# Sorting the second batch's k and v in natural layout, with crossbar transposes in place of TensorE's

**Chip, cores, metric.** One core of one Trainium2 chip. The metric is the device time of one execution in microseconds (us), median of the fast runs (a run over 1.5% above the fastest of its kernel counts as slow), and only fast runs are compared. The span in a profile is some 2 us shorter than the time.

## The reference

Four batches of eight heads: a Sinkhorn-normalised 8 x 8 matrix per head mixes the eight blocks of k and of v, then softmax attention runs inside each block of 96 rows; the result goes through a feed-forward network (FFN).

```python
# q, k, v: (4, 8, 768, 64); sort_net: (4, 8, 8, 8)
P = sinkhorn(sort_net)                                   # five rounds
k_sorted = einsum('bhij,bhjcd->bhicd', P, k_blocks)      # v the same
attn = softmax(q_blocks @ k_sorted^T / 8)                # within a block of 96
x = (attn @ v_sorted) -> (3072, 512)
out = relu(x @ w_in)**2 @ w_out                          # 512 -> 2048 -> 512
```

## The kernel before

The FFN runs in eight tiles of 384 tokens, two to a batch of heads. The attention of a batch runs, in four pairs of heads, between the FFN matmuls of the batch before. A planner on the host (`Plan`) lays all instructions in order of a time model; the order on TensorE (PE), VectorE (DVE), ScalarE (ACT) and the DMA issuer SP is fixed by it. The loads are issued by GpSimd (POOL); there the framework chooses the order, and an instruction waits only for what it needs, not for the plan's time.

Two forms of attention exist. Batches 1 and 2 (`u.b` 0 and 1) sort with full matrices on TensorE and transpose q and sorted v there, and x too, except for the first three of batch 2's four x. Batches 3 and 4 sort k and v in natural layout with 32 x 32 tiles of TensorE, send v through DRAM for its re-tiling, and transpose k, q and x by crossbar DMA:

```python
def load(b, t, h0, n, p=slice(0, 128)):          # GpSimd DMA, casts to bf16
    ...                                          # natural rows for b > 1 and k, v
    dma(..., readers[b - 2] + [x_done[b - 1, x, 0] for x in range(HP)] if b > 1 else [])
    # the second list is seen by the planner alone; the chip waits for the buffer only

def s_nat(b, g, t, due):                         # sort two head pairs in tiles   (L632)
    ...
    wr = plan.add("SP", 0.33, write, evs + [loaded(b)])   # v to DRAM             (L656)
    there = plan.add("WAY", 2.0, ...)
    rd = plan.add("SP", 0.33, read, [there] + oldw)       # and back, re-tiled    (L662)

def s_turn(b, hp):
    sp = plan.add("SP", 1.25, k_turn, [op, loaded(b)] + oldx)   # crossbar        (L683)
    k_op = plan.add("WAY", 1.6, ...)
    qp = plan.add("DVE", 0.5, q_pair, ...)                # qi: ring of two       (L695)
    sp = plan.add("SP", 1.25, q_turn, [qp, loaded(b)] + oldq)   # crossbar        (L706)

def s_xt(u, due=0, eng=AD):
    if u.b > 1 or u.b == 1 and u.hp < HP - 1:             # crossbar              (L764)
        ...
    # else: four or eight transposes on TensorE and a copy    (L779)
```

The softmax here doesn't subtract the row's maximum and nothing guards it: scores larger than these inputs give would overflow.

## Time and profile before

| | before |
|---|---|
| time, us | 226.5 (226.37 to 226.66) |
| span of the profile, us | 224.3 |
| TensorE busy | 216.6 us, 97% |
| granted TensorE clock | full throughout |
| last load of batch 3 / of batch 4 landed | 63.0 / 87.7 us |
| start of the third FFN tile (first of the second batch) | 82.7 us |

"Landed" means that the transfer's completion was signalled.

### The profile page before, as it was taken

Reading aid. Unit: us, or ns where it says so; the run is one execution under the profiler, and the core shown is the slowest. Engines: PE = TensorE matmul, PEld = TensorE weight load, DVE = VectorE, ACT = ScalarE, POOL = GpSimd, SP = SyncE. Lnnn points to the kernel's source line nnn. Section 1 sums busy time; section 2 is a strip of 40 time slices with the busy share of each in tenths; the row PEclk is TensorE's granted clock in tenths of the full one; section 3 lists DMA queues with packets and bytes.
Section 4 is the critical chain, followed back from the end, with each engine's and each line's share of the span. In section 5 each row is a group of like instructions: output and inputs, shape, how many; then the busy total and the mean of one; then the engine's idle time right before and its main releaser. Section 6 shows DMA issues by size and latency. Waiting matters only on the chain.

```text
span 224.3 us, 5245 instructions
## 1 busy us (share of the span) xinstructions
PE 216.6 (97%) x2130; PEld 122.9 (55%) x2145; DVE 105.7 (47%) x297; ACT 122.1 (54%) x253; POOL 26.4 (12%) x46
## 2 busy tenths in 40 slices
PE   7898999999999999999999999999999999999994
PEld 2476665556665645545665455445665465446553
DVE  6777777317666416640666127523664045005400
ACT  4665776228885328734775248535774177137521
POOL 7962332200004200000000000000000000000000
PEclk9999999999999999999999999999999999999999
DMA  5999999999953996499941320899522410110012
GB/s 66 201 202 208 207 206 205 203 227 245 210 65 27 191 239 145 115 216 201 220 38 35 85 94 0 164 225 254 110 37 43 122 47 1 50 57 37 0 50 94
DMA packets 42744, 28.83 MB, mean 129 GB/s; under 512 B 22752, under 2 KB 38368, under 8 KB 42720
## 3 DMA queue, kind: packets, MB, share of 16 engines
q0 software_dynamic: 13888, 13.63, 37.1%
q1 hardware_dynamic: 28832, 14.86, 29.7%
q8 instruction: 17, 0.28, 0.5%
q14 instruction: 7, 0.06, 0.1%
HBM read 28.89 MB, written 7.91 MB: 164 GB/s over the span
## 4 chain that ended last, share of the span: by engine, by line
PE 92%; DMA 2%; DVE 2%; ACT 1%; issue 1%; ACTq 0%; POOLq 0%
PE hp L810 37%; PE op L838 35%; PE p L550 4%; PE p L731 3%; DMA qb<-in_q_dram 2%; PE p L510 2%; PE qtp L461 2%; PE vbp L598 2%; PE op L872 2%; PE p L350 1%; PE p L632 1%; PE xtp L779 1%; PE tp L510 1%; DVE ao L742 1%; ACT h L818 0%
## 5 line engine op out<-in xcount | busy, mean ns | idle before, releaser
L810 PE MATMUL hp<-xT,w_in_bf 128*128 128x384 bf16 x512 | 91.0, 326 | 0.0
L838 PE MATMUL op<-w_out_bf,h 128*128 128x512 bf16 x353 | 82.6, 379 | 0.8
L818 ACT ACTIVATE h<-hp 128x384 bf16<-128x384 f32 x128 | 62.0, 495 | 23.5 <-PE hp L810 20.0
L821 DVE TENSOR_TENSOR h<-h 128x384 bf16<-128x384 bf16 x128 | 44.5, 355 | 56.3 <-ACT h L818 55.5
L810 PEld LDWEIGHTS <-w_in_bf 128*128 128x128 bf16 x512 | 47.0, 98 | 30.0 <-issue 0.7
L838 PEld LDWEIGHTS <-h 128*128 128x128 bf16 x368 | 34.7, 98 | 39.4 <-issue 0.7
L192 ACT COPY ob<-op 128x512 f32<-128x512 f32 (+1 forms) x25 | 14.2, 569 | 56.0 <-PE op L838 50.6
L742 DVE TENSOR_TENSOR ao<-p,rec 96x512 bf16<-96x512 f32 x32 | 22.0, 687 | 1.4 <-DVE rec L741 0.3
L582 ACT ACTIVATE et<-p 96x384 bf16<-96x384 f32 x48 | 19.4, 491 | 2.4 <-PE p L550 2.4
L741 DVE RECIPROCAL rec<-p 96x8 f32<-96x8 f32 x32 | 6.4, 199 | 13.6 <-PE p L731 13.3
L731 PEld LDWEIGHTS <-et 96*128 96x128 bf16 x256 | 10.6, 97 | 2.9
L261 POOL DMA_DIRECT2D qb<-in_q_dram x8 | 6.0, 754 | 32.5 <-PE qtp L461 24.4
L350 PE MATMUL p<-ones 128*128 128x512 bf16 (+1 forms) x36 | 8.8, 360 | 1.1 <-DVE ones L213 1.1
L194 DVE COPY vs<-vbp 96x512 bf16<-96x512 bf16 (+1 forms) x12 | 6.1, 508 | 7.1 <-PE vbp L598 6.9
L573 ACT ACTIVATE et<-p 96x768 bf16<-96x768 f32 x8 | 6.3, 802 | 2.1 <-PE p L550 2.0
L261 POOL DMA_DIRECT2D kb<-in_k_dram x10 | 6.6, 659 | 6.6 <-DMA w_in_bf<-in_moe_w_in_dram 2.2
L261 POOL DMA_DIRECT2D vb<-in_v_dram x10 | 6.6, 660 | 6.4 <-DMA w_in_bf<-in_moe_w_in_dram 3.6
L192 ACT CAST ksT<-p 128x768 bf16<-128x768 f32 (+1 forms) x7 | 4.6, 662 | 3.3 <-PE p L510 3.3
L550 PEld LDWEIGHTS <-kx 64*128 64x128 bf16 x128 | 4.6, 155 | 2.8 <-issue 2.8
L731 PE MATMUL p<-vs,et 96*128 96x65 bf16 x128 | 6.0, 193 | 0.0
L461 PE MATMUL qtp<-ident,qb 64*64 64x64 bf16 (+1 forms) x144 | 4.7, 204 | 1.3 <-DMA qb<-in_q_dram 1.3
L461 PEld LDWEIGHTS <-qb 64*64 64x64 bf16 (+1 forms) x144 | 3.5, 109 | 4.5 <-DMA qb<-in_q_dram 2.3
(78 smaller groups left out, 129.3 us busy)
## 6 DMA issues: line engine op xcount, KB each, us to landing
out_dram<-ob SPq DMA_DIRECT2D x23, 256.0 KB, 2.8
qb<-in_q_dram POOLq DMA_DIRECT2D x8, 384.0 KB, 15.7
vb<-in_v_dram POOLq DMA_DIRECT2D x6, 384.0 KB, 17.1
kb<-in_k_dram POOLq DMA_DIRECT2D x6, 384.0 KB, 17.1
w_in_bf<-in_moe_w_in_dram POOLq DMA_DIRECT2D x4, 512.0 KB, 12.5
w_out_bf<-in_moe_w_out_dram POOLq DMA_DIRECT2D x4, 512.0 KB, 18.0
v_way<-vn SPq DMA_DIRECT2D x4, 396.0 KB, 4.1
vblk<-v_way SPq DMA_DIRECT2D x4, 396.0 KB, 3.9
```

Source lines behind the costliest of these rows:

```text
L192: nc.scalar.copy(out=out, in_=in_)
L261: nc.gpsimd.dma_start(out=dst, in_=src)
L350: nc.tensor.matmul(out=out, lhsT=ones, rhs=rhs, start=True, stop=True)
L461: nc.tensor.transpose(out=t["p"][64 * h:64 * (h + 1), a, :], in_=qb[p0:p1, 2 * hp + h, D * a:D * (a + 1)], identity=ident[p0:p1, p0:p1])
L550: nc.tensor.matmul(out=scp[:, h, BLK * n:BLK * (n + 1)], lhsT=(u.ksT[64 * h:64 * (h + 1), hf, BLK * n:BLK * n + 128] if u.b < 2 else kx_r[ ...
L582: nc.scalar.activation(out=et[:, h, 0:HS].rearrange("p (n c a) -> p n c a", c=C0, a=NA), in_=st["p"][0:96, h, 0:HS].rearrange("p (n a c) - ...
L731: nc.tensor.matmul(out=oup[:, h, 66 * n:66 * n + D + 1], lhsT=et_r[u.et[hf]][:, h, BLK * n:BLK * n + 128], rhs=(u.vs[:, NQ * hf + n, h, 0: ...
L742: nc.vector.tensor_tensor(out=u.ao[:, n0:n0 + NQ, :, :].rearrange("p n e d -> p e n d"), in0=ov[:, :, :, 0:D], in1=rec[:, :, :, None].to_b ...
L810: nc.tensor.matmul(out=t["hp", nt][:, 0:HS], lhsT=w_in_bf[:, kc, 128 * nt:128 * (nt + 1)], rhs=xT[:, kc, t0:t0 + HS], start=(kc == 0), sto ...
L818: nc.scalar.activation(out=t["h1", nt], in_=t["hp", nt][:, 0:HS], func=AF.Relu)
L821: nc.vector.tensor_tensor(out=t["h2"][:, nt, :], in0=t["h1", nt], in1=t["h1", nt], op=ALU.mult)
L838: nc.tensor.matmul(out=t["op", mt], lhsT=t["h2"][:, nt, 128 * mt:128 * (mt + 1)], rhs=w_out_bf[:, nt, :], start=(nt == 0), stop=(nt == NT ...
```

## The change

Batch 2 joins the form of batches 3 and 4. The intent is to take its transposes and full sorts off TensorE, which bounds the kernel. The core of the diff:

```diff
-            if b > 1 and t:
+            if b > 0 and t:                 # natural rows for batch 2's k and v too
...
-            for t in (2, 1, 0):
+            for t in (1, 2, 0):
                 load(1, t, HP * g, HP)
...
-        if u.b > 1 or u.b == 1 and u.hp < HP - 1:
+        if u.b > 0:                         # every x of batch 2 by crossbar
...
-                if b == 1:
-                    build_w(H * b + 2 * hp, 2, pt, kops[b - 1, hp])
...
-    lay(1, (0, 1), n_up, 2 * n_up)
-    lay_late(2, 2 * n_up)
-    lay_late(3, 4 * n_up)
+    todo.append((8, len(todo), build_wt, 0))
+    lay_late(1, (n_up - 5, n_up + 1), n_up + 6, 5)
+    for b in (2, 3):
+        c0 = 2 * (b - 1) * n_up
+        todo.append((c0, len(todo), lambda due, b=b: load_late(b), 0))
+        lay_late(b, (c0 + 9, c0 + 18), c0 + 25, 6)
```

The rest is `u.b < 2` becoming `u.b < 1` in scores and attention, and a ring of four k buffers for three.

More of the change, by code (lines that the diff above doesn't have):

```diff
@@ L177 @@
     rqT, rao, rks, ret = Ring(6), Ring(3), Ring(3), Ring(4)
-    rkx, rkn, rqi = Ring(3), Ring(3), Ring(2)
+    rkx, rkn, rqi = Ring(3), Ring(4), Ring(2)
     AD = ("ACT", "DVE")
@@ L235 @@
     v_way = nc.dram_tensor("v_way", (B, 2, NA, 128, HP * 66), BF16, kind="Internal").ap()
-    kn_r = [const.tile([128, NA, 2, D], BF16, name=f"kn{n}") for n in range(3)]
+    kn_r = [const.tile([128, NA, 2, D], BF16, name=f"kn{n}") for n in range(4)]
     qi_r = [const.tile([128, NA, 2, D], BF16, name=f"qi{n}") for n in range(2)]
@@ L252 @@
     xT = const.tile([128, KC, n_tok], BF16)
-    w_all = const.tile([128, NH // 2, NB, C0], BF16)
+    w_all = const.tile([128, H, NB, C0], BF16)
     w_t = const.tile([128, NH // 4, 4, NB], BF16)
@@ L436, in __init__ @@
             self.b, self.hp, self.halves = b, hp, halves
-            if b > 1:
+            if b > 0:
                 self.i0, self.ni, self.full = 0, NB, True
@@ L544, in mm @@
                 qT = tiles["qT", u.b, u.hp]
-                if u.b < 2:
+                if u.b < 1:
                     qT = qT.rearrange("p a x -> p (a x)").rearrange("p (i q) -> p i q", q=BLK)
@@ L552, in mm @@
                             lhsT=(u.ksT[64 * h:64 * (h + 1), hf, BLK * n:BLK * n + 128]
-                                  if u.b < 2 else
+                                  if u.b < 1 else
                                   kx_r[u.kx][64 * h:64 * (h + 1), NQ * hf + n::NB]),
-                            rhs=(qT[64 * h:64 * (h + 1), NQ * hf + n, :] if u.b < 2 else
+                            rhs=(qT[64 * h:64 * (h + 1), NQ * hf + n, :] if u.b < 1 else
                                  qT[64 * h:64 * (h + 1), :, C0 * (NQ * hf + n):
@@ L561, in s_sc @@
             u.et[hf], olde = ret.take()
-            pe = plan.add("PE", 0.17 if u.b < 2 else 0.26, mm, [u.k_op, u.q_op] + old, due,
+            pe = plan.add("PE", 0.17 if u.b < 1 else 0.26, mm, [u.k_op, u.q_op] + old, due,
                           mode="row")
@@ L565, in s_sc @@
             rqT.use(qTs[u.b, u.hp], pe)
-            if u.b < 2:
+            if u.b < 1:
                 rks.use(u.n, pe)
@@ L716, in s_av @@
         nao, olda = rao.take()
-        if u.b > 1:
+        if u.b > 0:
             w, u.vs_op = v_blk[u.b, u.hp // 2]
@@ L733, in mm @@
                             lhsT=et_r[u.et[hf]][:, h, BLK * n:BLK * n + 128],
-                            rhs=(u.vs[:, NQ * hf + n, h, 0:D + 1] if u.b < 2 else
+                            rhs=(u.vs[:, NQ * hf + n, h, 0:D + 1] if u.b < 1 else
                                  vb_r[w][:, NQ * hf + n, 2 * (u.hp % 2) + h, 0:D + 1]),
@@ L753, in s_av @@
             ret.use(u.et[hf], pe)
-            if u.b < 2:
+            if u.b < 1:
                 rks.use(u.n, pe)
@@ L761, in s_xt @@
     def s_xt(u, due=0, eng=AD):
-        if u.b > 1 or u.b == 1 and u.hp < HP - 1:
+        if u.b > 0:
             def turn(e):
@@ L956, in lay, with lay_late @@
                 todo.append((c + step * f, len(todo), s, b))
-    def lay_late(b, c0):
-        todo.append((c0, len(todo), lambda due: load_late(b), 0))
-        if b == 2:
-            todo.append((c0, len(todo), build_wt, 0))
+    def lay_late(b, nat, c1, step):
         for g in range(2):
             for t in (1, 2):
-                todo.append((c0 + 9 + 9 * g, len(todo),
-                             lambda due, g=g, t=t: s_nat(b, g, t, due), b))
+                todo.append((nat[g], len(todo), lambda due, g=g, t=t: s_nat(b, g, t, due), b))
         for hp in range(HP):
@@ L973, in scores @@
                 s_sc(u, due)
-            c = c0 + 25 + 6 * hp
+            c = c1 + step * hp
             todo.append((c, len(todo), scores, b))
```

## The prediction

> **What bounds the kernel now.** I read the page's busy shares first, then the chain of waits.
>
> ```profile
> PE 216.6 (97%) x2130; PEld 122.9 (55%) x2145; DVE 105.7 (47%) x297; ACT 122.1 (54%) x253; POOL 26.4 (12%) x46
> PE 92%; DMA 2%; DVE 2%; ACT 1%; issue 1%; ACTq 0%; POOLq 0%
> ```
>
> TensorE is busy 97% of 224.3 us and carries 92% of the chain that ends last. VectorE and ScalarE stand near half. So a microsecond taken off TensorE's in-order stream is a microsecond off the time, and each new wait in that stream is paid in full. What the change removes are pieces of that stream. The chain in order of time (start, us, what) gives one head pair of the second batch, then its last output transpose and two pieces that the third batch has instead:
>
> ```profile
> 62.52 0.46 PE qtp L461 x12
> 62.98 0.34 PE p L510 x12
> 64.07 0.46 PE p L510 x12
> 65.28 0.28 PE p L550 x8
> 65.58 0.35 PE p L550 x8
> 66.69 0.45 PE vbp L598 x8
> 68.43 0.51 PE p L731 x16
> 77.86 0.34 PE xtp L779 x8
> 88.64 0.31 PE p L632 x16
> 102.85 0.63 PE p L550 x16
> ```
>
> Line 461 transposes q, 510 sorts k and v, 550 makes scores, 598 transposes v, 731 applies attention to v, 779 transposes the output. In the third batch 632 sorts in tiles, two head pairs to a piece.
>
> The second thing to know is what the DMA engines do where the change puts new transfers. GpSimd's timeline shows the last two loads that use the first batch's buffers, those of batch 3 of 4, already issued at 44 and 46 us, although the program's host-side plan puts them after the second batch:
>
> ```profile
> 43.73 0.53 POOL L261 DMA_DIRECT2D kb<-in_k_dram  x1 [1.12 <-DMA qb<-in_q_dram]
> 45.61 0.53 POOL L261 DMA_DIRECT2D vb<-in_v_dram  x1 [1.36 <-DMA vb<-in_v_dram]
> ```
>
> They land 17.2 and 17.4 us later, at 61 and 63 us. One crossbar transpose of the second batch is issued inside that time, at 56.5 us. The view of its line says when it landed, and the same view for the one at 63.4 us, with no load in flight:
>
> ```profile
> L764 SPq DMA_TRANSPOSE xT<-ao x1: 1312/1312/1312, 56.5 to 56.5; - x1
> DMA to landing us min/median/max: 7.1/7.1/7.1
> L764 SPq DMA_TRANSPOSE xT<-ao x1: 1915/1915/1915, 63.4 to 63.4; - x1
> DMA to landing us min/median/max: 3.0/3.0/3.0
> ```
>
> The stretches of half a microsecond (the last column is GB/s, the one before it the DMA engines' share) show where its 197 KB went:
>
> ```profile
> 60.50:61.00 0.50, 0.50 (x5) 0.29 (x3) 0.50 (x2) 0.39 (x2) 0.00 (x0) 1.00 1.07 208
> 61.50:62.00 0.50, 0.50 (x14) 0.41 (x11) 0.44 (x3) 0.39 (x1) 0.00 (x0) 1.00 1.30 139
> 62.00:62.50 0.50, 0.50 (x6) 0.14 (x5) 0.50 (x1) 0.00 (x0) 0.00 (x0) 1.00 1.16 91
> 62.50:63.00 0.50, 0.50 (x21) 0.50 (x22) 0.47 (x3) 0.44 (x1) 0.00 (x0) 1.00 0.99 122
> ```
>
> From 57 to 61.5 us the rate stays near the loads' 210 GB/s. From 61.5 to 63 it is 139, 91 and 122, which is (139+91+122) x 0.5 = 176 KB: at most a little less than the whole transpose, moved once the loads had ended. A transpose beside loads gets a small share. One at 70.5 us, beside the fourth batch's loads, took 6.8 us. Output stores take 5.3 to 6.6 us beside loads and 2.3 to 3.9 without.
>
> **What the Trainium skill says.** "DMA: Bandwidth & Descriptors", section "Issuing engines are not separate DMA queues": DMAs of all issuers run on the same 16 engines and interleave. The 7.1 us against 3.0 us agrees. The same page, "Queues, rings and completion order": an engine goes round its queues packet by packet, so a queue of small packets gets few bytes beside one of large packets. The rates above fit. "Perfetto Trace Analysis", section on the HWDGE DMA instruction: the profiler's duration there leaves out the data movement. The trace agrees: 1.31 us shown, 7.1 us to landing. "TensorE: Matmul & The Clock Gate", "The HAM clock gate": after some 3.4 us idle the clock halves, until about as long a busy stretch. The trace before has no such gap (clock 9 in all slices), so no run shows it yet.
>
> **The change, part by part**, over the second batch's four head pairs.
> - Removed from TensorE, from the chain: q transposes 4 x 0.46 = 1.84; k and v sorts 0.67 + 0.80 + 0.80 + 0.80 = 3.07; v transposes 0.55 + 0.45 + 0.45 + 0.55 = 2.00; the last output transpose 0.34. Sum 7.25 us.
> - Added: tiled sorts as in the third batch, 0.31 + 0.31 + 0.31 + 0.53 = 1.46; scores in the strided form 4 x 0.63 = 2.52 in place of 0.45 + 0.63 + 0.63 + 0.45 = 2.16, so 0.36. Net on TensorE: 7.25 - 1.46 - 0.36 = **5.4 us less**. Building the tiled weights only moves earlier.
> - Off the path: VectorE loses four weight builds (4 x 0.42 us); eviction work of some 3 us per head pair becomes some 2. Neither engine bounds.
> - Added on the DMA engines: two v writes and two reads of 396 KB, eight more k and q transposes and one more x transpose. In the third batch, with no load in flight, the transposes take 2.8 to 5.7 us to land and v 3.4 to 6.0 us each way.
>
> Where these fall decides. The first v write sits after the first FFN tile's stores, at about 50.4 us (the third store is issued at 50.1, the second batch's last load lands at 50.0). K and q transposes of head pair 0 follow by 53.4 us. The plan wants its scores six FFN chunks into the second tile: tile start 49.5 + 0.6 for two tiled sorts + 6 x 0.65 + 0.6 for the other two = about 54.6 us. Unloaded, q would land near 56, a wait of 1 to 1.5 us. But at 50.4 us there are some 11 us of batch-3 loads in flight, and batch 4's k and v loads may follow at once, since their buffers are now free after the sorts (about 51 us) and not at 70 us as before. My estimate of a transpose's time in the queue is 5 us beside loads (7.1 - 3.0 more than its unloaded 1.3), and 4 us for the v write: write done 55.5, k 60.5, q 63 to 65.5, landing 1.5 later: 64.5 to 67 us. TensorE, in order, waits some 10 to 12 us at the first scores. VectorE waits with it, as it does before now for a q copy buffer (5.5 us in the waits), and the FFN's squares stand behind that. Head pair 1's q queues behind the v read, and costs another 1 to 3; the end of the batch, with its last x now through DMA (four down chunks of 0.87 = 3.5 us from attention's start, against 0.5 + 1.3 of normalising + 3.4 of transpose) another 1 to 1.5. An idle of 10 us also drops the clock: half speed for 3.4 us, about 1.7 us. Sum: 226.4 - 5.4 + 11 + 2 + 1.3 + 1.7 = 237 us if loads interfere fully. If the share is fairer (half that first wait, little after), 226.4 - 5.4 + 6 + 3 + 1 = 231.
>
> **The rivals.**
> - *The gain comes through.* The plan's order hides all transfers: 226.4 - 5.4 = 221.0, or 222.5 with the 1.5 us wait at the batch's end. For it: batches 3 and 4 run in this form with no TensorE wait at all in the waits of 88 to 180 us. Against: batch 3's first scores come at 102.8 us, six microseconds after its q landed, with the loads over at 87.5 us; here there is neither slack nor quiet.
> - *Loads interfere* (my choice, 231 to 240). For: 7.1 and 6.8 us beside loads, against 3.0. Against: only two transposes show it, and how several in a row share is not seen.
> - *It cancels*: waits of 4 to 7 us for 5.4 saved, 225 to 229. This is so if GpSimd's queue holds batch 4's loads back behind the q load, whose buffer frees late, and small packets get their turn.
>
> **Range and chances.** I put 0.12 on the gain coming through to over 2% (under 221.9 us), 0.30 on within 2%, 0.58 on over 2% slower (over 231). Weighing 221, 227 and 237 so, the middle lies near **233 us**, and 221 to 243 should hold it 8 times in 10.
>
> **What would show it.** Right: TensorE busy time down by some 5 us if the clock holds; rows of lines 461 (the 128-row ones), 598 and 779 gone or fewer; a TensorE wait on the k or q transposes between 54 and 70 us; landing times of those transposes of 6 us and more; a clock dip there. Wrong: landing near 3 us between 50 and 60 us, no wait at line 550, or batch 3's loads no longer in flight after 50 us. Then 221 is the time. If TensorE waits on the v read instead, the mechanism holds and the carrier was another transfer.

## The result, and the profile after

247.4 us median of four runs (244.6 to 248.0) against 226.5 before: a ratio of 1.090 (95% interval 1.083 to 1.097), slower. Ratios here are the mean time of one kernel's fast runs over that of the other's of the same rounds, so not quite the ratio of the medians. The profiled one (244.6) is the quickest of the four, so its lines show a little less than the typical loss.

Busy times, chain and clock from the page of the changed kernel:

```profile
PE 217.8 (90%) x2025; PEld 120.1 (50%) x2025; DVE 101.3 (42%) x289; ACT 121.0 (50%) x252; POOL 25.6 (11%) x46
PE   8998999995008987999999999999999999999994
PEclk9999999999555799999999999999999999999999
PE 73%; DMA 11%; DVE 5%; SPq 5%; ACT 2%; issue 2%; POOL 1%; POOLq 0%; DVEq 0%; ACTq 0%
```

The hole in TensorE's row is at the slices of 6 us that read 5, 0, 0 and 8; the clock is at half in and after it. TensorE's share of the chain fell from 92% to 73%, and DMA and the DMA issuer took its place. The chain in order of time (start, us, what) through that stretch:

```profile
52.55 9.70 SPq L683
62.25 0.05 issue
62.29 10.52 DMA qT<-qi
72.81 0.04 issue
72.85 0.86 PE p L550 x16
...
81.94 10.32 DMA qT<-qi
92.25 0.14 issue
92.39 0.70 PE p L550 x16
...
97.93 2.80 DMA xT<-ao
```

The issue of the first k transpose alone took 9.70 us on SP, where a k transpose of the kernel before took 1.2 to 1.5, and the q transpose behind it landed at 72.8 us. The first scores stood until then. The waits of TensorE:

```profile
PE p L550 <- DMA qT<-qi: 17.4, 2, 15.1
```

Two waits, 15.1 us and 2.3 us. The loads are in GpSimd's timeline, batch 4's k and v first and its q much later:

```profile
52.40 1.05 POOL L261 DMA_DIRECT2D kb<-in_k_dram  x2 [6.66 <-PE p L632]
54.12 1.06 POOL L261 DMA_DIRECT2D vb<-in_v_dram  x2 [0.66 <-PE p L632]
80.80 1.50 POOL L261 DMA_DIRECT2D qb<-in_q_dram  x2 [25.62 <-DVE qi L695]
```

The views of single DMA lines, with time to landing; the first pair is the v write, then the k and the q transpose of head pair 0, then the two v loads of batch 4:

```profile
L656 SPq DMA_DIRECT2D v_way<-vn x1: 438/438/438, 52.1 to 52.1; - x1
DMA to landing us min/median/max: 19.5/19.5/19.5
L683 SPq DMA_TRANSPOSE kx<-kn x1: 9696/9696/9696, 52.6 to 52.6; - x1
DMA to landing us min/median/max: 19.6/19.6/19.6
L706 SPq DMA_TRANSPOSE qT<-qi x1: 6379/6379/6379, 62.3 to 62.3; - x1
DMA to landing us min/median/max: 10.5/10.5/10.5
L261 POOL DMA_DIRECT2D vb<-in_v_dram x2: 531/534/538, 54.1 to 54.6; - x2
DMA to landing us min/median/max: 15.3/16.1/16.8
```

The last load landed at 54.6 + 16.8 = 71.4 us. The v write landed at 71.6, k at 72.2, q at 72.8: one behind the other, only when the loads had ended, although they had been issued 10 to 20 us before.

The trace also keeps every DMA packet with its time, queue and size, which no view above prints. Counted by queue, they show what happened between issue and landing. From 58 to 69 us the loads' queue (GpSimd's) and SP's queue each finished 66.5 packets a us: one for one. The loads' data packets are of 3072 bytes, the v write's of 528, so the loads moved 182 GB/s and SP's queue 35. The v write's 768 packets began at 57.7 us, when the output stores ahead of them on SP's queue were all but through, and ended at 70.4; the k transpose behind them moved its first packet at 69.3.

The second wait is the same event again: batch 4's q loads, issued at 80.8 and 81.5 us, landed at 91.7 at the latest, and the last q transpose of batch 2, issued at 81.9, landed at 92.2.

The third FFN tile begins at 99.6 us and not at 82.7: 16.9 of the 18.2 us that the span grew.

### The profile page after: what moved, and what is told of

Same layout as the page of the kernel before. It is cut to its first block, busy times and chain, and to the rows that moved or that the text cites. A ratio compares the mean times of both kernels' runs of the same rounds, so it can differ in the third digit from the quotient of the medians.

```text
span 242.5 us, 5040 instructions
## 1 busy us (share of the span) xinstructions
PE 217.8 (90%) x2025; PEld 120.1 (50%) x2025; DVE 101.3 (42%) x289; ACT 121.0 (50%) x252; POOL 25.6 (11%) x46
## 4 chain that ended last, share of the span: by engine, by line
PE 73%; DMA 11%; DVE 5%; SPq 5%; ACT 2%; issue 2%; POOL 1%; POOLq 0%; DVEq 0%; ACTq 0%
PE hp L810 32%; PE op L838 28%; DMA qT<-qi 10%; SPq L683 4%; PE p L550 3%; PE p L731 3%; DVE ao L742 2%; PE p L632 2%; PE op L872 1%; DMA xT<-ao 1%; PE vbp L598 1%; PE tp L510 1%; PE xtp L779 1%; PE p L510 1%; DVE rec L741 1%
## 5 line engine op out<-in xcount | busy, mean ns | idle before, releaser
L810 PE MATMUL hp<-xT,w_in_bf 128*128 128x384 bf16 x512 | 93.6, 333 | 0.5 <-DMA xT<-ao 0.5
L838 PE MATMUL op<-w_out_bf,h 128*128 128x512 bf16 x368 | 83.8, 379 | 0.0
L810 PEld LDWEIGHTS <-w_in_bf 128*128 128x128 bf16 x512 | 48.2, 99 | 32.9 <-issue 4.2
L582 ACT ACTIVATE et<-p 96x384 bf16<-96x384 f32 x48 | 19.5, 491 | 20.6 <-PE p L550 20.6
L550 PE MATMUL p<-qT,kx 64*128 64x96 bf16 x192 | 9.0, 231 | 17.5 <-DMA qT<-qi 17.4
L550 PEld LDWEIGHTS <-kx 64*128 64x128 bf16 x192 | 7.4, 155 | 21.9 <-DMA kx<-kn 14.9
L695 DVE COPY qi<-qb 128x768 bf16<-128x768 bf16 x12 | 4.0, 354 | 27.9 <-DMA qT<-qi 27.9
L350 PE MATMUL p<-ones 128*128 128x512 bf16 (+1 forms) x36 | 10.0, 399 | 1.1 <-DVE ones L213 1.1
L731 PE MATMUL p<-vblk,et 96*128 96x65 bf16 x192 | 8.7, 197 | 0.6 <-ACT h L818 0.6
L194 DVE CAST kn<-p 128x768 bf16<-128x768 f32 x6 | 5.7, 957 | 7.9 <-PE p L632 7.9
L192 ACT CAST kn<-p 128x768 bf16<-128x768 f32 x6 | 4.8, 796 | 5.7 <-PE p L632 5.7
## 6 DMA issues: line engine op xcount, KB each, us to landing
kb<-in_k_dram POOLq DMA_DIRECT2D x6, 384.0 KB, 16.8
vb<-in_v_dram POOLq DMA_DIRECT2D x6, 384.0 KB, 16.9
```

Source lines behind the costliest of these rows:

```text
L192: nc.scalar.copy(out=out, in_=in_)
L350: nc.tensor.matmul(out=out, lhsT=ones, rhs=rhs, start=True, stop=True)
L550: nc.tensor.matmul(out=scp[:, h, BLK * n:BLK * (n + 1)], lhsT=(u.ksT[64 * h:64 * (h + 1), hf, BLK * n:BLK * n + 128] if u.b < 1 else kx_r[ ...
L582: nc.scalar.activation(out=et[:, h, 0:HS].rearrange("p (n c a) -> p n c a", c=C0, a=NA), in_=st["p"][0:96, h, 0:HS].rearrange("p (n a c) - ...
L731: nc.tensor.matmul(out=oup[:, h, 66 * n:66 * n + D + 1], lhsT=et_r[u.et[hf]][:, h, BLK * n:BLK * n + 128], rhs=(u.vs[:, NQ * hf + n, h, 0: ...
L810: nc.tensor.matmul(out=t["hp", nt][:, 0:HS], lhsT=w_in_bf[:, kc, 128 * nt:128 * (nt + 1)], rhs=xT[:, kc, t0:t0 + HS], start=(kc == 0), sto ...
```

## The experiments

Twelve kernels ran. "Held back" means a true dependency: a one-column copy on GpSimd from the awaited tile into the load's own buffer, ahead of the load. All gave correct results.

### x1: no loads of batch 4 beside batch 2

```diff
+            if b in (3,):
+                nc.gpsimd.tensor_copy(out=qkv[b][t][:, h0, 0:1],
+                                      in_=tiles["qT", b - 1, HP - 1][:, 0, 0:1])
```

> The changed kernel, with the fourth batch's loads held back until the second-to-last batch's (the third batch's) last q transpose has landed; the third batch's loads stay in flight. Theory (new transfers move nearly nothing while loads are in flight): the v write, k and q transposes of head pair 0 land when the third batch's last load lands, near 63 us and not 72; the first TensorE wait shrinks from 15 to about 7 us, and the late q transpose at 82 us no longer takes 10 us. Time about 236 (233 to 239). Rival (the new transfers are slow by themselves, by their own queueing on one issuer): the first wait stays near 15 us and the time at 244 or more.

Measured: 234.2 us median of three fast runs (the fourth, 239.3, counts as slow), ratio 1.035 (1.032 to 1.038). SP's timeline and TensorE's wait:

```profile
52.73 7.25 SPq L686 DMA_TRANSPOSE kx<-kn  x1
60.03 2.98 SPq L709 DMA_TRANSPOSE qT<-qi  x1
PE p L553 <- DMA qT<-qi: 7.3, 1, 7.3
```

The last load of batch 3 landed at 63.0 us; the v write at 63.8, k at 64.5, q at 65.2. The wait is 7.3 us, as expected, and the second one is gone. Landing follows the end of the loads wherever that is put; a delay from queueing on the issuer alone would not have moved with it.

### x2: no loads beside batch 2's k, q and v transfers

The same with `b in (2, 3)`.

> The changed kernel with the loads of both the third and the fourth batch held back until the last q transpose of the batch before has landed, so no load is in flight beside the second batch's new transfers. Theory: transposes land in 3 to 5 us, the first wait is under 2 us, no dip of the clock, and the saving on TensorE of 5.4 us comes through: 221 to 223.5 us. Rival (queueing by themselves): still above 235. Second rival (the plan leaves too little slack even without loads): 225 to 230, with waits at scores or at the end of the batch.

Measured: 239.1 us, ratio 1.056. The theory's first half held: the v write, k and q of head pair 0 landed in 5.6, 5.4 and 4.2 us and the first scores waited 0.8 us. The time did not follow, because the loads of batch 3, let go by the last q transpose at 71.4 us, now met batch 2's x transposes:

```profile
PE hp L813 <- DMA xT<-ao: 10.6, 4, 5.8
```

The same interference, moved to the next transfer. My second rival named waits at the end of the batch. They came, but from loads and not from a tight plan, and the time missed its 225 to 230.

### x3: the same holds in the kernel before

> The kernel before with the same two holds, as a control. Theory: its loads were hidden and its second batch needs only three crossbar transposes, so the time stays at 226.4, within 0.5 us. If it gets faster by several us, the hold helps by itself and x2 is no evidence for the change.

Measured: 226.2 us, ratio 0.9995 (0.998 to 1.001). Holding loads back does nothing for the kernel before, so what it does in the others belongs to the change.

### x4: a warm clock

```diff
                 st["p"] = scp = p2[slot]
+                if u.b == 1 and u.hp == 0 and hf == 0:
+                    fill(0.33 * 68, slot)     # 68 matmuls in the hole
```

> The changed kernel with 68 filler matmuls (about 14.7 us at full clock) put before the first scores of the second batch, where TensorE stands idle; nothing else changed, results unaffected. Theory: the clock stays full, and the 8 us of half speed after the wait, worth about 4 us, are saved: about 243 to 244 us against 247.4. Rival (the half clock is hidden behind other waits there): no change within 1 us. If the filler outlasts the wait, the time could not fall.

Measured: 246.6 us median of three fast runs (the fourth counts as slow), ratio 1.085: no gain clear of the noise, though the clock stayed full through the hole. The late scores of head pair 3 in the timeline of the changed kernel, then of x4:

```profile
92.39 0.70 PE L550 MATMUL p<-qT,kx 64*128 64x96 bf16 x16 [2.27 <-DMA qT<-qi]
```

```profile
92.76 0.86 PE L552 MATMUL p<-qT,kx 64*128 64x96 bf16 x16 [4.17 <-DMA qT<-qi]
```

TensorE came to them earlier and waited longer, for a transpose whose landing is set by batch 4's q loads; and in that longer wait the clock fell to half after all, from 91.8 to 98.6 us. So x4 alone doesn't say what the clock is worth.

### x8 and x9: only batch 4's q loads held back, without and with the filler

x8 has x1's hold with `and t == 0` (q alone); x9 is x8 with x4's filler.

> The changed kernel with only the fourth batch's q loads held back (until the third batch's last q transpose has landed); its k and v loads follow at once as in the changed kernel. Theory: the first wait stays at 15 us, the last q transpose of the second batch, issued near 82 us, lands in 3 to 4 us instead of 10, and the wait of 2.3 us at 92 us goes: 243 to 245. Rival (that late transpose is slow for another reason): 247.

> x8 with the 68 filler matmuls of x4. x4 kept the clock full after the first wait and gained nothing; my reading is that the time won was waited away again at the last q transpose, whose landing at 92 us is set by the fourth batch's q loads. Theory: with those loads out of the way the clock's 4 us show: 239 to 241, 3 to 4 us under x8. Rival (the half clock costs nothing anyway): equal to x8 within 1 us.

Measured: x8 243.0 us (ratio 1.072), x9 241.4 (1.066). Holding q back takes the second wait away, about 4 us of time (2.3 of them by the start of the third tile). The third FFN tile begins, in x8 and in x9:

```profile
97.30 0.65 PE L813 MATMUL hp<-xT,w_in_bf 128*128 128x384 bf16 x3
```

```profile
96.31 0.65 PE L815 MATMUL hp<-xT,w_in_bf 128*128 128x384 bf16 x3
```

So with the second wait out of the way the clock is worth 1.0 us by the third tile and 1.6 us in time, not the 4 us that I had put on it: TensorE, earlier now, waited longer for the v read (1.6 us for 0.7), and around it the clock still stood at half for 3.4 us (75.7 to 79.1), so this is the least that it is worth.

### x5, x6, x7: quiet for all of batch 2's transfers

x5 holds both batches' loads back for the last x of the batch before (`in_=xT[:, HP - 1, S * b - 1:S * b]`). x6 also lets batch 2's transfers stand early in the plan; x7 also puts the last x back on TensorE:

```diff
     def loaded(b):
-        return [landed[b, t, HP, 0] for t in (0,)][0]
+        return landed[b, 0, HP, 0] if b > 1 else None      # x6
...
-        if u.b > 0:
+        if u.b > 1 or u.b == 1 and u.hp < HP - 1:          # x7
```

> As x2, but each held-back batch of loads waits until the last x transpose of the batch before has landed (and not its last q transpose), so that the second batch's x transposes have quiet too. x2 stayed at 239 because its loads, let go at 71.6 us, met the second batch's x transposes: 10.6 us of waits on them. Theory: those waits shrink to 1 to 2 us and the clock stays full; the time falls by 8 to 13 us to 226 to 230. What stays are waits in the first half (1 to 2 us at the first scores, 1.6 us at the first v read) and slower FFN chunks around them. Rival (the x waits come from the plan's tightness, not from loads): still above 235.

> As x5, and the second batch's transposes and v writes no longer wait, in the plan's order, for its last load: the first v write stands on the issuer ahead of the third store of the first FFN tile, which alone costs it some 3 us in x5. Theory: waits at the first scores and the first v read vanish, 222.5 to 225. Rival: the transposes then run beside the second batch's own last loads (to about 49 us) and are held as before, so nothing is gained, or it is worse than x5.

> As x6, and the second batch's last x is transposed on TensorE, as in the kernel before. It costs 0.34 us of TensorE and takes away the transfer of some 2.8 us ahead of the third FFN tile. If that transfer is waited for (1 to 1.5 us), this is 0.5 to 1.2 us faster than x6; if it is hidden, 0.3 slower.

Measured: x5 234.2 us (ratio 1.035), x6 232.4 (1.026), x7 233.0 (1.030). In x5 the waits on x shrank to 0.6 us as expected, yet I had expected 226 to 230. TensorE's waits in x6 and the start of its third tile, then that start in the kernel before:

```profile
PE hp L813 <- ACT h L821: 5.6, 3, 4.2
78.80 0.65 PE L813 MATMUL hp<-xT,w_in_bf 128*128 128x384 bf16 x3
```

```profile
82.68 5.96 PE hp L810 x36
```

Batch 2 now works: the third tile starts 3.9 us earlier. But loads held until x come too late for the batches they feed. VectorE, in order, stood 2.3 and 6.0 us for q loads of batches 3 and 4 before its pair copies; the FFN's squares stood behind those copies, ScalarE's evictions waited for the squares, and TensorE for ScalarE. So x6 missed its 222.5 to 225. x7 was not faster than x6.

### x10, x11, x12: the loads in the gaps between transfers

x10 is x6 with batch 3's k and v let go by batch 2's last q transpose, batch 3's q and batch 4's k and v by batch 2's last x, and batch 4's q by batch 3's last x. x11 is x10 with the last x on TensorE. x12 is x11 with batch 3's q let go together with its k and v.

> As x6 (second batch's transposes early), but the loads are put into the gaps between the transposes and not behind each batch: the third batch's k and v wait for the second batch's last q transpose, its q and the fourth batch's k and v for the second batch's last x, and the fourth batch's q for the third batch's last x. In x6 the third FFN tile began 3.9 us earlier than in the kernel before (78.8 against 82.7 us), but the held-back loads came too late and TensorE waited 5.6 us for what hangs on them. Theory: those waits go, the head start stays, 222.5 to 224.5, that is 1 to 2% under the kernel before. Rival (the loads collide with the second batch's x transposes or the third batch's first transposes instead): 226 or more.

> As x10, with the second batch's last x transposed on TensorE. In x6 the third tile waited 0.57 us on that transfer, after three matmuls; the transpose on TensorE costs 0.34. Theory: within 0.5 us of x10, rather faster. The loads that hang on this x start some 3 us earlier too.

> As x11, but the third batch's q loads go with its k and v, right after the second batch's last q transpose, and only the fourth batch's k and v follow the second batch's last x (made on TensorE); all other engines' programs are the same. In x11 the fourth batch's loads (let go at 78.8 us behind the third's q) still ran when the third batch's first q transpose was issued at 89.9 us, and it held the chain for 9.4 us. Theory: those loads end near 87 us, the third batch's transposes find quiet, and some 1 to 2 us more come off: 223 to 224.3. Rival: the second batch's first three x transposes, issued between 62.6 and 71.6 us, are now held to about 77 us and come too late for the third tile at 78.9: 225 or more.

Measured: x10 226.3 us, ratio 1.002 (0.999 to 1.005); it missed its 222.5 to 224.5, and the time is its rival's. x11, which I had expected within 0.5 us of it, has **224.9 us, ratio 0.994 (0.992 to 0.996)**: the one version under the kernel before, though inside the 2% that count as the same. x12 has 227.3 us over its fast runs, ratio 1.001; three of its six runs count as slow, up to 234.9, and why they spread so is not shown. The third tile of x11, then the line in its chain that takes the head start back; then the third tile of x12, going on after two matmuls at 79.3 us:

```profile
78.88 6.01 PE L818 MATMUL hp<-xT,w_in_bf 128*128 128x384 bf16 x36
89.85 9.39 DMA qT<-qi
```

```profile
83.44 7.37 PE L818 MATMUL hp<-xT,w_in_bf 128*128 128x384 bf16 x34 [3.62 <-DMA xT<-ao]
```

x11's first q transpose of batch 3, issued at 89.9 us, landed at 99.2, held by batch 4's loads (let go at 78 us, landed by 95.4). x12 moves those loads earlier, and the same thing happens to batch 2's x transposes instead: the one issued at 72.1 us took 11.3 us, and the third tile waited 3.6 us. Batch 3's k and q transposes then landed in 2.8 to 4.3 us. Its rival was right. The packets of this third kind of meeting show the same: from 74 to 81 us the loads' queue and SP's moved 996 and 994 packets, and until 78 us, with x's of 256 bytes, SP's got 33 GB/s beside 167.

## Why the prediction was wrong

The direction and the cause it named, loads in flight, held; the measured 247.4 lies over the stated range of 221 to 243.

- **TensorE's saving, 5.4 us net.** Supported. In x11 the third tile starts 3.8 us early in spite of 0.34 us for the x kept on TensorE and 0.6 us of waiting: 4.7 us accounted for. (Over the whole run x11's TensorE is busy 2.6 us less, 214.0 for 216.6, and not some 5, the sign that I had named; I did not place the rest.)
- **Loads in flight hold the new transfers back, batch 4's among them.** Right: batch 4's k and v were issued at 52 to 54 us. x1 moves the landing with the loads, x2 and x5 bring it to 5.6 us and less, x3 shows that the holds do nothing by themselves.
- **A transpose's time beside loads, estimated at 5 us, and 4 us for the v write: this is the term that failed.** A v write's packets took 12.7 us beside loads (57.7 to 70.4), for 1.7 in x2 without any (53.7 to 55.4), with one packet of the loads finished for each of them; and the transposes behind it on SP's queue moved nothing before 69.3. From issue to landing the three took 19.5, 19.6 and 10.5 us, all ending within 1.4 us of the last load. So the first wait is the loads' remaining time, 71.4 us less the 57.7 at which TensorE stopped, plus 1.4: 15.1 us and not 10 to 12.
- **The lines that this estimate was read from.** "A small share" was not what the transpose of 56.5 us showed. By its packets it moved nothing for 3.8 us, then 67 of its 197 KB before 61.5 us. Of the 176 KB after that, 52 were the loads' own. That small packets get few bytes beside large ones was right, but only the packet counts above show it. (Of the six stores beside loads one took 4.9 us, less than the 5.3 to 6.6 named.)
- **What comes after the first wait, 1 to 3 us and the batch's end.** The first size was about right (2.3 us) by luck: the carrier was not the v read but batch 4's q loads, which VectorE's own pair copy lets go at just that moment, and which my sum did not have. x8 shows it. The end of the batch cost about 0.6 us of wait for x after three matmuls.
- **The clock, 1.7 us.** Half speed lasted far longer than the 3.4 us that I had given it after the wait (from 72.9 to 81.3 us), but most of it lay beside other waits: at least 1.6 us by x8 and x9, and in x4 nothing that the second wait did not take back.
- **The sum.** Between the second tile's start (50.6 before, 50.9 after) and the third's, the stretch grew from 32.1 to 48.7 us, by 16.6. The 5.1 us saved there (5.4 less the 0.3 that falls before that mark), set against 15.1 and 2.3 of waits, leave 4.4 us (16.6 + 5.1 - 15.1 - 2.3, rounded from finer figures). About 1 of it is the clock, by x8 and x9; that the rest is FFN chunks slowed around the waits by VectorE and ScalarE is my reading and not shown.
- **The middle of 233** came from weighing three outcomes (which gives 232). Even the case that happened stood at 237 in my sum. The range ended too near it for a size drawn from two transposes.

What stays open: why a newly issued transfer starts so late beside loads (3.8 us from issue to first packet for the transpose of 56.5 us, 1.2 for the one of 63.4 with no load in flight). The packet records do not name the DMA engine, so one for one is a count over all of them. The rest of the head start in x11, some 2 us, is lost in batch 3, where the chain runs through a transpose that stood beside batch 4's loads; no order that I tried gave every transpose quiet. Not tried: the v write or the stores on another issuer's queue, so that the transposes need not stand behind their packets.

## What to carry to other kernels

A transfer that was harmless when nothing depended on it becomes the bound when a new short transfer on the critical path has to share the DMA engines with it: before moving work from a compute engine to DMA, list what bulk loads are in flight at that time on the chip, not in the plan. Then count packets and not bytes: those ahead on the same queue and the transfer's own, each paying for one packet of the loads, until the loads end. At 66.5 packets a us the 1536 packets of the first k and q alone would have needed 23 us (an estimate from the count above), so here the end of the loads came first and set the delay. And freeing a buffer earlier starts the next load earlier: check what it will collide with.

## What the Trainium skill lacked or had wrong

- "DMA: Bandwidth & Descriptors", section "Queues, rings and completion order": it says that an engine goes round its queues packet by packet. The trace agrees (66.5 packets a us from each of two queues). What it lacks is the consequence in bytes: packets of 528 bytes got 35 GB/s beside 182 for packets of 3072, and a transfer of 768 of them took 12.7 us for 1.7 alone.
- The same page, section "Rules for kernel authors", says that a transpose next to ordinary DMAs needs nothing. This holds for correctness (all twelve kernels were correct), but it should add the cost in time: 19.6 us from issue to landing, part of it behind a v write, against 5.4 with the loads held back (x2).
- "Perfetto Trace Analysis", section on the HWDGE DMA instruction: it says that the profiler's duration of an issue leaves out the data movement. Beside loads the issue does not stay short either: one transpose's lasted 9.70 us and the next 6.38, against 1.2 to 1.5 us in the kernel before, and held everything behind it on that issuer. The page draws a wait for a lock and a buffer that fills, without a duration; which of them this was is not shown.
- "TensorE: Matmul & The Clock Gate", section "The HAM clock gate": half clock after about 3.4 us of idle is near (3.1 us here, from 57.7 to 60.8). The return came 8.5 us after the first matmul at 72.9 us and 5.3 after the start of unbroken work at 76.0, so the page's 3.4 us of sustained work is the least to reckon with. In these traces the times between changes of the clock are whole multiples of 3.413 us (54.61 and 20.48 here, 3.413 and 10.24 in x2).
